# A scan and a mixture of adapters: a written order of every engine in place of a planner's, with deeper rings

## The chip, the cores and the metric

The kernel runs on one core of a Trainium2 chip. The time is that of the device, in microseconds, for one execution from inputs in HBM to the output in HBM. The profile is of one execution, and its span runs from the first to the last instruction of the program.

The engines are named as in the profile: PE (TensorE, matmuls and transposes), PEld (its weight loads), DVE (VectorE), ACT (ScalarE), POOL (GpSimd) and SP (SyncE, which issues the DMAs here). Each has a queue of its own that runs strictly in order, and they meet only through semaphores.

## What is computed

```python
# a, b: (8, 6400, 128), f32; 51200 rows of 128 in all
h = 0                                   # for each of the 8 batches
for t in range(6400):
    h = a[:, t] * h + b[:, t]
    x[:, t] = h
x = x.reshape(51200, 128)
logits = x @ w_gate                     # w_gate (128, 8)
topk = two largest logits of each row   # weights: softmax over the two
delta = sum over the two e of  weight * (x @ A[e]) @ B[e]   # A (8,128,16), B (8,16,128)
out = x + delta
```

## The kernel before

The 51200 rows are cut into 100 units of 512 rows. A unit goes through these operations, named by letter and unit in the code:

- **lda, ldb** (SP): loads of a and b, 512 KB for two units, into rings of 8 slots (16 units); a pairs units 2k-1 and 2k, b pairs 2k and 2k+1. A load waits until the transposes of the units that held its slot are done.
- **AB** (PE, line 86): 8 + 8 transposes of a and b, f32 with half of the array, into PSUM tiles pA (one buffer) and pB (two). The units 0, 1 and 99 have them in two halves, A and AB.
- **aev** (ACT, line 491): pA to SBUF (a_st). **scan** (DVE, line 510): the recurrence along the free dimension, from a_st and pB into xT, a ring of XR = 16 units in f16, transposed (128 features on the partitions).
- **L** (PE, line 82): logits, into a part of the PSUM tile pTL. After a group of up to four units **lev** (ACT, line 583) takes them out, and the gating chain **m1, p1, p2, p3, m2, p4, p5, p6, p7** (DVE for m, POOL for p) and **sig** (ACT, line 684) makes the weights g. The first three groups have a short form (mx, p4, p1, p5, p6, p7) whose p steps may run on POOL or DVE.
- **Z** (PE, pZ), **mul** (DVE, line 729; 21 of 100 on POOL after a copy **zev** by ACT): x A, times the weights, into zw.
- **T** (PE, into the other part of pTL) and **tev** (ACT, line 786): zw transposed, in zwT (4 units).
- **R** and **D** (PE, pO, two buffers): x by the identity, plus zwT by B, added up in one PSUM tile.
- **oev** (ACT, line 821; for the last ten units ACT or DVE): pO into outt, a ring of NOUT = 24 slots.
- **st** (SP): stores of 512 KB for a pair, numbers 2 to 48; the units 0, 1 and 96 to 99 have stores of 256 KB, numbers 0, 1 and 49 to 52. Store j of a pair holds the units 2j-2 and 2j-1. A store waits for its oev, and, where its first unit u is below 78, for the scan of unit u + 22 (HOLD, FREE).

The order of each queue is made when the kernel is built: `_Plan.schedule` is a list scheduler with costs in nanoseconds for each operation, a table of offsets (KEY) that sets priorities, and a slack for each engine. From about unit 24 on, the order that it makes on PE is regular: `AB60 T48 L58 D46 Z51 R47 AB61 T49 ...`, so T runs 12 units behind AB, D 14 and R 13. On DVE a round of four units is `scan mul scan mul m scan mul scan m`. On SP each pair of loads is followed by one store once stores begin (store 0 after the load of b for unit 38). Its last part is `ldb98 st31 lda99 st32 st33 st34 st35 st36 st40 st37 st41 st42 st38 st43 st39 st44 ... st52`. The last queue entry waits for all stores of the end.

The waits that an operation has are kept with it (`deps`), and `_Plan.run` writes for each a wait on the semaphore of the engine that it needs, its own engine included. Two of them bear on the change:

```python
[f"AB{w}", f"aev{w}"] + [f"scan{w - 1}"] + [f"{k}{v}" for v in mates(w - XR) for k in "RDZL"]   # scan
[f"D{v}", f"st{store_of.get(v - NOUT)}"]                                                        # oev
```

## Time and profile before

| | |
|---|---|
| three runs, us | 204.41, 206.39, 206.44 (median 206.39) |
| the profiled execution, us | 204.88 |
| its span, us | 203.1 |
| instructions | 8757 |
| HBM read and written, MB | 52.56 and 26.21 |
| mean granted TensorE clock | 0.989 |
| scan (DVE), each | 1252 ns, 96 whole ones |
| product (DVE) / product (POOL), each | 679 / 1060 ns |
| evacuations by ACT: aev, tev, oev, each | 606, 615, 626 ns |

Busy times of DVE and ACT contain the last part of an instruction in which the next one has begun, so that the durations add up to more than the time they take in a row. Busy PE is modelled in the profile, as its matmuls are pipelined: what counts there is when the next instruction begins and whether it waited.

### The profile page before, as it was taken

The numbers are of one execution on the slowest core, as the hardware profiler recorded it, in microseconds if no ns is written. First come the engines' busy times: TensorE is split into PE (matmuls) and PEld (weight loads), VectorE is DVE, ScalarE is ACT, GpSimd is POOL, SyncE is SP. The second block draws the span as 40 slices with busy tenths as digits, with TensorE's granted clock in tenths as the row PEclk, the third lists the DMA queues.
The fourth block names the chain that finished last, engine by engine and source line by source line (L and its number), as shares of the span: only waits on it lengthen the run. The fifth ranks groups of instructions, "written<-read, shape, count | busy, mean of one in ns | idle before, by whom it ended". The sixth has DMA issues, their size and how long they took to land.

```text
span 203.1 us, 8757 instructions
## 1 busy us (share of the span) xinstructions
PE 191.2 (94%) x3591; PEld 172.3 (85%) x3591; DVE 184.8 (91%) x268; ACT 173.7 (86%) x383; POOL 115.7 (57%) x244
## 2 busy tenths in 40 slices
PE   7788888999999999999999999999999999999992
PEld 3666777879899999999999999999999999999981
DVE  1579989999999999999999999999999999989970
ACT  3157686869899999989999999999999999999883
POOL 1324427568567466565656746656565687875520
PEclk9799999999999999999999999999999999999999
DMA  7999999999999999999999999999999999988867
GB/s 182 402 410 408 403 409 405 404 412 404 404 414 412 416 412 410 413 408 416 414 408 416 410 412 416 410 414 414 409 411 414 414 416 409 372 330 345 324 250 279
DMA packets 23688, 79.35 MB, mean 391 GB/s; under 512 B 3681, under 2 KB 3809, under 8 KB 23649
## 3 DMA queue, kind: packets, MB, share of 16 engines
q1 hardware_dynamic: 22320, 78.65, 97.0%
q8 instruction: 29, 0.48, 0.9%
q10 hardware_dynamic: 1328, 0.14, 0.5%
q14 instruction: 11, 0.08, 0.1%
HBM read 52.56 MB, written 26.21 MB: 388 GB/s over the span
## 4 chain that ended last, share of the span: by engine, by line
PE 81%; DVE 6%; ACT 6%; DMA 2%; issue 2%; POOL 1%; SPq 0%; DVEq 0%
PE pA L86 26%; PE pO L82 23%; PE pTL L86 14%; PE pZ L82 10%; PE pTL L82 5%; DVE xT L510 4%; PE pB L86 4%; DMA a_in<-in_a_dram 2%; ACT a_st L491 2%; ACT outt L821 2%; ACT zwT L786 1%; DVE mx L589 0%; SPq L311 0%; DVE zw L729 0%; ACT z_sb L715 0%
## 5 line engine op out<-in xcount | busy, mean ns | idle before, releaser
L510 DVE TENSOR_TENSOR_SCAN xT<-a_st,xT,pB 128x512 f16<-128x512 f32 x96 | 120.2, 1252 | 4.4 <-PE pZ L82 1.1
L491 ACT COPY a_st<-pA 128x512 f32<-128x512 f32 x100 | 60.6, 606 | 20.4 <-PE pB L86 15.7
L86 PE MATMUL pA<-ident_f,a_in 64*128 64x64 f32 (+1 forms) x792 | 71.8, 230 | 3.3 <-DMA a_in<-in_a_dram 1.1
L86 PE MATMUL pB<-ident_f,b_in 64*128 64x64 f32 (+1 forms) x792 | 72.5, 232 | 0.2
L86 PEld LDWEIGHTS pA<-ident_f,a_in 64*128 64x128 f32 (+1 forms) x792 | 58.0, 139 | 11.6 <-issue 2.4
L821 ACT COPY outt<-pO 128x512 f32<-128x512 f32 x96 | 59.5, 626 | 1.9 <-PE pO L82 1.7
L786 ACT COPY zwT<-pTL 128x512 f16<-128x512 f16 x95 | 58.4, 615 | 1.0 <-PE pTL L86 1.0
L86 PEld LDWEIGHTS pB<-ident_f,b_in 64*128 64x128 f32 (+1 forms) x792 | 58.0, 140 | 0.7 <-DMA b_in<-in_b_dram 0.4
L729 DVE TENSOR_TENSOR zw<-pZ,g 128x512 f16<-128x512 f32 x79 | 53.2, 679 | 2.1 <-PE pTL L86 1.2
L82 PE MATMUL pO<-ident_h,xT 128*128 128x128 f16 x400 | 41.2, 229 | 0.9 <-ACT outt L821 0.9
L82 PE MATMUL pZ<-cst_h,xT 128*128 128x128 f16 x400 | 38.6, 221 | 0.0
L86 PE MATMUL pTL<-ident_h,zw 128*128 128x128 f16 x380 | 37.7, 222 | 0.4 <-ACT zwT L786 0.4
L82 PE MATMUL pO<-cst_h,zwT 128*128 128x128 f16 x400 | 36.9, 218 | 0.6 <-ACT zwT L786 0.4
L82 PEld LDWEIGHTS pO<-ident_h,xT 128*128 128x128 f16 x400 | 32.8, 148 | 1.6 <-ACT outt L821 1.2
L729 POOL TENSOR_TENSOR zw<-z_sb,g 128x512 f16<-128x512 f32 x21 | 22.3, 1060 | 17.6 <-PE pTL L82 17.2
L82 PE MATMUL pTL<-cst_h,xT 128*128 128x8 f16 x400 | 27.9, 175 | 1.6 <-DVE xT L510 1.3
L82 PEld LDWEIGHTS pZ<-cst_h,xT 128*128 128x128 f16 x400 | 28.1, 115 | 0.2
L86 PEld LDWEIGHTS pTL<-ident_h,zw 128*128 128x128 f16 x380 | 21.8, 98 | 6.4 <-ACT zwT L786 0.5
L82 PEld LDWEIGHTS pTL<-cst_h,xT 128*128 128x128 f16 x400 | 23.6, 117 | 2.9 <-DVE xT L510 1.8
L625 POOL TENSOR_TENSOR d<-Lg,m 128x128 f32<-128x128 f32 (+3 forms) x29 | 10.7, 368 | 26.6 <-DVE m L618 26.5
L82 PEld LDWEIGHTS pO<-cst_h,zwT 128*128 128x128 f16 x400 | 23.9, 98 | 1.0 <-PE pO L82 0.9
L660 POOL TENSOR_SCALAR pn<-d 128x128 f32<-128x128 f32 (+3 forms) x31 | 17.3, 557 | 2.7
(36 smaller groups left out, 137.2 us busy)
## 6 DMA issues: line engine op xcount, KB each, us to landing
a_in<-in_a_dram SPq DMA_DIRECT2D x49, 512.0 KB, 13.7
b_in<-in_b_dram SPq DMA_DIRECT2D x49, 512.0 KB, 13.5
out_dram<-outt SPq DMA_DIRECT2D x47, 512.0 KB, 13.1
out_dram<-outt SPq DMA_DIRECT2D x6, 256.0 KB, 2.7
a_in<-in_a_dram SPq DMA_DIRECT2D x2, 256.0 KB, 9.2
b_in<-in_b_dram SPq DMA_DIRECT2D x2, 256.0 KB, 4.3
cst_f<-in_moe_A_dram ACTq DMA_DIRECT2D x1, 64.0 KB, 4.0
cst_f<-in_moe_B_dram ACTq DMA_DIRECT2D x1, 64.0 KB, 5.0
```

What stands on the lines that cost most here:

```text
L82: return self.h.matmul(*args, **kw)
L86: return self.h.transpose(*args)
L491: lambda h: h.copy(a_st[w % 2][:, :], pA[0][:, :]),
L510: last = h.tensor_tensor_scan(out=x_at(lo, hi), data0=a_st[w % 2][:, lo:hi], data1=pB[w % 2][:, lo:hi], initial=init, op0=ALU.mult, op1=AL ...
L625: lambda h: h.tensor_tensor(out=v(d1[s]), in0=v(Lg[s]), in1=bc(m1[s]), op=ALU.subtract),
L660: lambda h: h.tensor_scalar(v(pn[s]), v(d2[s]), 0.0, -1.0e30, ALU.is_lt, ALU.mult),
L729: lambda h: h.tensor_tensor(out=oview, in0=zview, in1=gview, op=ALU.mult),
L786: lambda h: h.copy(*evacuated(v)),
L821: return copy(outt[:, v % NOUT, :], pO[v % NO][:, :])
```

## The change

The scheduler goes, with its costs, offsets and slacks. In its place stand five strings with a letter for each operation, one for each engine, and two that give the order in which the users of the PSUM tiles pA and pTL hold them. The n-th letter of a kind is the n-th operation of that kind.

```diff
-KEY = {
-    "AB": -228.9, "aev": 79.1, "scan": 140.1, "L": -12.2, "lev": -63.6, "gate": 83.5, "sig": 69.7, "Z": 27.8,
...
+ORDERS = {
+    "pe": """
+        hAaAaLaLZaZRaZLLaTRLaZTaDLaTaZDLLLaZaTRaZaTDLRaDRLLLaTRLZaDZTaDTZLaRLLDaRZDaTLLRaZTLRaLDTZaZDRTaRZLT
...
+    "sp": """
+        jiijjijjijiiiijjijjjjijiijjiijiiijjiiijjjjiiwwjijiijwijwwjjjiiwiiwwiwiwijjiwiwjiijjjijjjwwwwwiwjjiiii
+        wijiwijwiwwwwwjjjjjiijwijwiwwwwwjwjwiwwwwwwwwwwwwwwwwwwe
+    """,
 }
...
+ELSE = "oev90 oev94 oev97 oev98 oev99 p4_0 p5_0 p5_1".split()
...
-XR = 16
-NOUT = 24
+XR = 20
+NOUT = 36
...
+    def arrange(self):
+        ops = list(self.ops.values())
+        for op in ops:
+            op.deps = [self.ops[d] for d in dict.fromkeys(op.deps) if d in self.ops]
+        self.order = {e: self.pick(ORDERS[e], [op for op in ops if op.eng == e]) for e in self.sems}
...
-        zwT = [sb(nc.sbuf_tensor(f"zwT{i}", [128, 2 * UT], F16)) for i in range(2)]
+        zwT = [sb(nc.sbuf_tensor(f"zwT{i}", [128, 4 * UT], F16)) for i in range(2)]
...
-            deps = [f"aev{w - 1}", f"scan{w - 2}", "id"]
+            deps = [f"aev{w - 1}", f"scan{w - 2}", "id", "heat"]
...
-                [f"T{v}"] + [f"D{w}" for w in mates(v - 4)],
+                [f"T{v}"] + [f"D{w}" for m in mates(v) for w in mates(m - 8)],
...
-        plan.schedule(700.0, 3000.0, lambda t: 400.0, 94.0)
+        plan.arrange()
```

The letters of PE: h the heating matmuls, A and a the transposes, the others as above; of SP: i lda, j ldb, w a store. ELSE names the operations that may run on two engines and run on DVE here: the evacuations 90, 94, 97, 98 and 99 (before: 90, 92, 94 and 97) and the gating steps p4_0, p5_0 and p5_1 (before: p7_0, p7_1, p7_2 and p5_2). The 21 products on POOL are those of the same units, now in a list.

Read with their numbers, some parts of the new orders:

- PE, beginning: `heat A0 AB0 A1 AB1 L0 AB2 L1 Z0 AB3 Z1 R0 AB4 Z2 L2 L3 AB5 T0 R1 L4 AB6` (before: `heat A0 AB0 A1 L0 AB1 Z0 R0 AB2 L1 Z1 R1 AB3 L2 AB4 T0 Z2 AB5 L3 D0 AB6`).
- PE, middle: `AB40 D24 R25 Z30 T28 L37 L38 AB41 D25 R26 Z31 T29 L39 L40 AB42 R27 D26 T30 D27 Z32 Z33 AB43 R28 L41 T31 D28 AB44`.
- DVE, beginning: `scan0 scan1 mx_0 p4_0 p5_0 scan2 mx_1 mul0 scan3 p5_1 scan4 mx_2 mul1` (before: `scan0 mx_0 scan1 p7_0 scan2 mul0 mx_1 scan3 p7_1 scan4 mul1 mx_2`).
- DVE, end: `scan98 mul88 m1_30 mul89 mul90 mul91 m2_30 scan99 mul92 mul93 m1_31 oev90 mul94 mul95 m2_31 mul96 mul97 oev94 mul98 mul99 oev97 oev98 oev99` (before: `mul88 m2_29 scan97 mul89 mul90 m1_30 scan98 mul91 m2_30 scan99 mul92 mul93 m1_31 oev90 mul94 mul95 m2_31 oev92 mul96 mul97 oev94 mul98 mul99 oev97`).
- ACT, end: `oev93 sig31 tev96 oev95 tev97 oev96 tev98 tev99` (before: `oev93 tev96 tev97 sig31 oev95 oev96 tev98 tev99 oev98 oev99`).
- SP: the first loads are b, then a, of unit 0 (before a, then b). Loads and stores come in runs: `lda71 ldb68 ldb70 ldb72 st12 st13 st14 st15 st16 lda73 st17`, `lda87 ldb80 st20 lda89 st21 st22 st23 st24 st25 ldb82 ldb84 ldb86 ldb88 ldb90`. The end is `lda97 st28 ... st32 ldb96 st33 ldb98 st34 lda99 st35 st36 ... st52`, the stores in the order of their numbers.

## The prediction

> **What bounds the kernel now.** The page comes first, for the share of each engine and for the chain of waits.

> ```profile
> span 203.1 us, 8757 instructions
> PE 191.2 (94%) x3591; PEld 172.3 (85%) x3591; DVE 184.8 (91%) x268; ACT 173.7 (86%) x383; POOL 115.7 (57%) x244
> PE 81%; DVE 6%; ACT 6%; DMA 2%; issue 2%; POOL 1%; SPq 0%; DVEq 0%
> ```

> TensorE, VectorE and ScalarE are all near full, and 81% of the chain runs on TensorE. An average hides the stages, so the busy time by stretches is next. Its columns are the stretch and its length, busy time (instructions) of each engine, the granted clock, the share of the DMA engines and the GB/s.

> ```profile
> 0.00:5.00 5.00, 3.63 (x12) 1.52 (x13) 0.56 (x3) 1.66 (x3) 0.89 (x7) 1.00 0.70 179
> 5.00:10.00 5.00, 3.92 (x42) 3.38 (x44) 3.04 (x7) 1.09 (x3) 1.61 (x6) 0.76 1.03 401
> 10.00:50.00 40.00, 35.25 (x669) 30.37 (x666) 37.57 (x63) 29.23 (x67) 20.41 (x49) 0.99 1.03 407
> 50.00:180.00 130.00, 129.84 (x2576) 119.86 (x2574) 127.35 (x170) 123.95 (x274) 83.83 (x161) 1.00 1.02 410
> 180.00:190.00 10.00, 9.84 (x169) 9.15 (x170) 9.29 (x14) 9.45 (x23) 6.22 (x16) 1.00 0.87 346
> 190.00:203.06 13.06, 8.72 (x136) 8.01 (x136) 6.98 (x13) 8.35 (x18) 2.72 (x8) 0.97 0.69 266
> ```

> From 10 to 50 us VectorE is the fuller engine (2.43 us idle) and PE idles 4.75 us. From 50 to 180 us PE idles 0.16 us and VectorE 2.65 us. The DMA engines run at 407 to 410 GB/s until 180 us and then slacken. The waits of the middle stage, and the beginnings of the transposes of two neighbouring units, say which engine sets the pace there.

> ```profile
> POOL d L625 <- DVE m L618: 20.5, 17, 1.5
> POOL zw L729 <- PE pTL L82: 16.7, 17, 1.1
> ACT a_st L491 <- PE pB L86: 5.2, 20, 0.6
> DVE xT L510 <- ACT a_st L491: 0.4, 2, 0.2
> 100.27 0.27 PE L86 MATMUL pA<-ident_f,a_in 64*128 64x64 f32 x1
> 102.08 0.27 PE L86 MATMUL pA<-ident_f,a_in 64*128 64x64 f32 x1
> ```

> The same view kept to PE lists no wait at all between 50 and 180 us; the others wait for PE. A unit takes 102.08 - 100.27 = 1.81 us, and 100 units make 181 us. So the span of 203.06 us is about 181 us of PE issue, and 22 us of beginning, of stalls up to 50 us, and of the end. DMA needs this:

> ```profile
> q1 hardware_dynamic: 22320, 78.65, 97.0%
> out_dram<-outt SPq DMA_DIRECT2D x47, 512.0 KB, 13.1
> out_dram<-outt SPq DMA_DIRECT2D x6, 256.0 KB, 2.7
> ```

> 78.65 MB at 410 GB/s are 191.8 us, so DMA is nearly as tight as PE. A last store of 256 KB takes 2.7 us, of which 0.262 MB at 410 GB/s are 0.64, so about 2.06 us are fixed.

> **The change, part by part.** No operation is added or removed on PE, ACT or SP except that a few evacuations and gating steps change engine; the same 21 products stay on POOL. What moves is the order, and the depth of three rings. So the middle cannot gain while PE issues 1.81 us a unit without a wait. What can move is the beginning, the stalls, and the end.

> *Beginning.* These are VectorE's first rows.

> ```profile
> 5.61 1.22 DVE L510 TENSOR_TENSOR_SCAN xT<-a_st,pB 128x512 f16<-128x512 f32 x1 [3.88 <-PE pB L86]
> 8.07 0.37 DVE L589 MAX8 mx<-Lg 128x8 f32<-128x8 f32 x4 [1.25 <-ACT Lg L583]
> 8.50 1.28 DVE L510 TENSOR_TENSOR_SCAN xT<-a_st,xT,pB 128x512 f16<-128x512 f32 x1
> 9.76 0.19 DVE L674 TENSOR_TENSOR um<-d,pn 128x32 f32<-128x32 f32 x1
> 11.08 1.28 DVE L510 TENSOR_TENSOR_SCAN xT<-a_st,xT,pB 128x512 f16<-128x512 f32 x1 [1.13 <-PE pZ L82]
> ```

> Two gaps, 1.25 and 1.13 us, stand before scan 1's max and before scan 2. Today PE runs L0 between A1 and the second half of unit 1, and Z0, R0 ahead of AB2. The new order runs A1, AB1, L0, AB2, and only then L1 and Z0; VectorE runs scan 0 and scan 1 back to back and then mx_0. That takes Z0 and R0 out of the way of scan 2. Against it stand the swap of the first two loads and the new wait of A0 for the end of the heating matmuls: both delay scan 0 (A0 and B0, now one after the other behind the second load; 0.262 MB at 410 GB/s put that load 0.64 us behind). Scan 0 has the 1.25 us gap behind it, so this is covered; without the gap it would cost those 0.64 us. The steps p4_0, p5_0 and p5_1 come to VectorE and p7_0 to p7_2 and p5_2 leave it, at 0.19 us each by the row of p7: 0.19 us less work. The bounds of the whole head are a loss of 0.64 and a gain of 2.38 us (both gaps); I take half the gaps, 1.2 us, since the next loads are still only landing then.

> *Middle.* The written order is less regular: groups of two to five L stand together, and R and D come in pairs. On PE a stall is lost time, as every other engine waits for it. A loss of 0 is the bound from the row 50 to 180 us (0.16 us idle); the other is the idle share of 10 to 50 us, 4.75 in 40, which over 130 us would be 15.4 us. The same operations with the same distances between producer and user (T still runs 12 units behind AB) are near the first, and x of 20 units instead of 16 loosens the one wait that was tight: scan w waits for R, D, Z and L of units w-16 and w-15, and D45 stands today right before AB60. I take a loss of 0.6 us, about one stall.
> [...]

> *Loads and stores.* SP's queue is in order, so each DMA waits for what stands before it. The tightest new place is the load of b for unit 82. It now stands behind a's load for unit 89, which needs AB74 done, and behind stores 20 to 25. From AB74 to AB82 are 8 x 1.81 = 14.5 us; lda89, six stores and the load itself are 8 x 0.524 MB, 10.2 us at 410 GB/s, plus 2.06 us. It lands with some 2 us to spare: nothing, as long as the queue is empty when it starts; with one more store ahead of each it would cost up to a unit. 36 slots instead of 24 cost and bring nothing by themselves: no ACT wait for a store stands among the waits, and oev v now waits for the store of v-36.

> *End.* These rows are VectorE's, with POOL and ScalarE where the last gate comes from.

> ```profile
> 185.83 1.27 DVE L510 TENSOR_TENSOR_SCAN xT<-a_st,xT,pB 128x512 f16<-128x512 f32 x1
> 188.01 1.28 DVE L510 TENSOR_TENSOR_SCAN xT<-a_st,xT,pB 128x512 f16<-128x512 f32 x1
> 189.20 1.26 DVE L729 TENSOR_TENSOR zw<-pZ,g 128x512 f16<-128x512 f32 x2
> 194.29 0.32 POOL L674 TENSOR_TENSOR um<-d,pn 128x64 f32<-128x64 f32 x1
> 195.27 0.60 ACT L786 COPY zwT<-pA 128x512 f16<-128x512 f16 x1
> 195.74 0.28 ACT L684 ACTIVATE g<-um 128x64 f32<-128x64 f32 x1
> 196.05 1.29 DVE L729 TENSOR_TENSOR zw<-pZ,g 128x512 f16<-128x512 f32 x2 [0.74 <-ACT g L684]
> 197.70 0.69 DVE L821 COPY outt<-pO 128x512 f32<-128x512 f32 x1 [0.35 <-PE pO L82]
> 199.36 0.58 ACT L821 COPY outt<-pO 128x512 f32<-128x512 f32 x1 [0.16 <-PE pO L82]
> ```

> The last gate (sig 31) waits in ACT's queue behind tev96 and tev97 although its input is there at 194.61; in the new order it stands before tev96. VectorE also loses oev92 before the last products and takes oev98 and oev99 behind them. The products of units 98 and 99 waited 0.74 us for the gate: that goes (-0.7), and the last evacuation takes 0.69 instead of 0.58 us (+0.1). Together -0.6 us.

> A new order of stores ends with 35, 36 ... 52. Store 39 holds units 76 and 77 and waits for scan 98 (HOLD 22); today 40 to 43 go ahead of it or beside it, in the new order 39 to 52 all stand behind that wait. These are ten of 512 KB and four of 256 KB, 6.29 MB, 15.3 us at 410 GB/s, plus 2.06 us: the end cannot come before scan 98's end + 17.4 us. Scan 98 ends today at 185.83 + 1.27 = 187.10, and the span 16.0 us later, so with scan 98 where it is this would cost 1.4 us. But VectorE's new order has mul88, mul89, mul90 and m1_30 behind scan 98 that stand before it today, 3 x 0.63 (half a row of two) + about 0.19 = 2.1 us. So scan 98 is at 187.1 - 2.1 - 1.2 + 0.6 = 184.4 us.

> **Sum.** By the engines: 203.06 - 1.2 + 0.6 - 0.6 = 201.9 us. By the stores: 184.4 + 17.4 = 201.8 us. The profiled execution took 204.88 us for its span of 203.06, 1.82 us more; 201.8 + 1.82 = 203.6 us. The profiled time is 0.7% below the median of 206.39 and near the lowest of the three (204.41), so against the median this is 1.4% less, and against the profiled execution 0.6%.

> **The rivals.** *Nothing is won.* The head gives nothing, as the loads set it, and the stores take the end: 187.1 - 2.1 + 0.6 + 17.4 = 203.0 us, 204.8 us in time. For it: DMA's share of 1.03 from 5 us on. Chance 0.22.

> *VectorE closes its gaps.* If PE's modelled 100% is not a limit, deeper rings let VectorE run on: its 2.65 us of idle time in 50 to 180 us go, and the loss of 0.6 does not come: 203.06 - 1.2 - 2.65 - 0.6 = 198.6 us, 200.4 us in time. For it: weight loads busy 119.86 of 130 us. Against it: PE's empty list of waits. [...] Chance 0.15.

> *Slower: PE stalls in the middle.* Its place is PE's queue between 50 and 180 us: an operation stands ahead of its input, and all behind it wait. The chain of the written order crosses engines that are 95% (ACT) and 98% (VectorE) busy there, so a late evacuation is not made up. At 0.46 us in 10, a bit under half of what 10 to 50 us show (4.75 in 40), the price is 6.0 us: 203.06 - 1.2 - 0.6 + 6.0 = 207.3, 209.1 us in time. It decides from 1.8 us on, the saving of head and end. Chance 0.23.

> **How the numbers follow.** The forecast has 0.40. Within 1% is what a measurement of this kernel cannot tell from no change, since its three runs lie 1% apart; faster by 1% is under 204.3, slower over 208.5 us. The forecast's 203.6 lies 0.7 us inside faster: 0.30 of its 0.40 there, 0.10 within. VectorE's rival gives 0.15 faster; the one of no gain 0.03 faster, 0.19 within. The stalls give 0.19 slower and 0.04 within, as a price of 3 us would be 206.1. Moving 0.01 to slower for a load that comes late, that is 0.48, 0.32 and 0.20. The range goes from 199.8 (the second rival, with a little more of the head) to 208.6 us (most of the stalls); it leaves out some 0.1 at either end.

> **What would show it.** Right: VectorE's gaps before scans 1 and 2 shrink by about 1.2 us; PE idles under 1 us between 50 and 180 us with a unit still at 1.81 us; scan 98 ends near 184.4 us; SP issues stores without a pause behind it, at about 410 GB/s; products 98 and 99 wait no longer for the gate. Wrong: PE waits listed in the middle; a unit under 1.79 us; loads of b near unit 82 awaited by PE; a DMA rate in the last 17 us below 380 GB/s.

## The result, and the profile after

The changed kernel takes **206.12 us** (median of 20 runs, 205.03 to 209.6) where the kernel before, run beside it on the same chip, takes 204.41 us (median of 20, 204.18 to 206.44). The ratio of the mean times is 1.0069, with a 95% interval of 1.0040 to 1.0097; it leaves out the three longest runs of the changed kernel (208.27 to 209.60 us), which fell in a slower state of the chip. That is slower, by less than the 1% that the prediction called no change, but not by nothing. The forecast was 203.6 us. The 206.39 us that it was measured against was the median of only three runs: of the 20 here, three lie at 206.4 us and the others from 204.2 to 204.9. Against 204.41 us the forecast was 0.4% less, a change inside the prediction's own band of no change. The profiled execution took 205.23 us, 0.35 us more than that of before.

These are lines of the page of the changed kernel:

```profile
span 203.4 us, 8803 instructions
PE 191.5 (94%) x3591; PEld 171.9 (85%) x3591; DVE 184.2 (91%) x268; ACT 177.5 (87%) x383; POOL 115.9 (57%) x245
PE 87%; DMA 3%; ACT 3%; DVE 3%; issue 2%; SPq 1%; DVEq 0%
```

The busy times are within 1 us of those of before, but for ScalarE's, which is 3.8 us more; the chain lies still more on PE (87% for 81%), with 3% of DMA in it (2% before). The busy time by stretches, with the columns that the prediction explains, shows where things moved:

```profile
5.00:10.00 5.00, 4.02 (x45) 3.23 (x45) 2.77 (x7) 2.79 (x6) 0.29 (x1) 0.89 1.04 405
10.00:50.00 40.00, 36.70 (x708) 32.15 (x706) 39.43 (x65) 31.58 (x71) 22.75 (x57) 0.97 1.03 407
50.00:180.00 130.00, 128.68 (x2531) 118.12 (x2529) 124.12 (x169) 124.54 (x270) 82.31 (x156) 1.00 1.02 406
180.00:190.00 10.00, 9.94 (x178) 9.33 (x177) 9.22 (x14) 9.53 (x22) 6.83 (x19) 1.00 0.77 301
190.00:203.40 13.40, 8.77 (x136) 7.93 (x135) 8.07 (x14) 7.79 (x18) 2.84 (x8) 1.00 0.85 329
```

From 10 to 50 us VectorE idles 0.57 us in place of 2.43, and PE 3.30 in place of 4.75: the beginning did get shorter. From 50 to 180 us PE idles 1.32 us in place of 0.16: something was lost there. The waits of PE in that stage, which were an empty list before, are now this one, and the timeline of PE has its place (start, duration, instruction, and in brackets the idle time before it):

```profile
PE pA L119 <- DVE xT L433: 1.2, 1, 1.2
```

```profile
151.81 0.25 PE L119 MATMUL pA<-ident_f,a_in 64*128 64x64 f32 x1 [1.16 <-DVE xT L433]
```

The instruction is the first transpose of unit 82. The view names VectorE, but the scan that the transposes wait for, that of unit 80, had ended at 150.23 us; the load of b for units 82 and 83 landed at 151.68 us, 0.13 us before the transposes began. Here is the queue ahead of it, in SP's timeline (neighbours of one kind are one line, with their count at the end):

```profile
133.36 0.33 SPq L287 DMA_DIRECT2D a_in<-in_a_dram  x1
133.74 0.44 SPq L287 DMA_DIRECT2D b_in<-in_b_dram  x1
134.28 0.41 SPq L287 DMA_DIRECT2D out_dram<-outt  x1
136.97 0.33 SPq L287 DMA_DIRECT2D a_in<-in_a_dram  x1
137.40 2.78 SPq L287 DMA_DIRECT2D out_dram<-outt  x5
140.22 3.88 SPq L287 DMA_DIRECT2D b_in<-in_b_dram  x5
```

Each transfer reports sixteen completions in the trace; the last of them is its landing, and these are worked out from there:

| transfer | lda87 | ldb80 | st20 | lda89 | st21 | st25 | ldb82 |
|---|---|---|---|---|---|---|---|
| issued, us | 133.36 | 133.74 | 134.28 | 136.97 | 137.40 | 139.49 | 140.22 |
| landed, us | 140.11 | 141.37 | 142.67 | 144.25 | 145.56 | 150.46 | 151.68 |

When lda89 is issued, five transfers are still under way (lda85, st19, lda87, ldb80 and st20), and from lda87 on every next one lands 1.2 to 1.6 us after the one before it. So ldb82 is not late by its own cost but by its place in a line that is never empty. A later run has the same order of SP with most of the stores' bytes left out (stores 2 to 48 light, below): there ldb82 lands 5.19 us after its issue, where it takes 11.45 here, and nothing waits for it.

At the end, SP issues as predicted, from 184.42 us on, when scan 98 has ended (184.35 us; the prediction had 184.4):

```profile
184.42 15.72 SPq L287 DMA_DIRECT2D out_dram<-outt  x14
```

The DMA issues after 198.4 us, with their size and the median time from issue to landing, first of before, then of after:

```profile
out_dram<-outt SPq DMA_DIRECT2D x3, 256.0 KB, 2.3
```

```profile
out_dram<-outt SPq DMA_DIRECT2D x3, 256.0 KB, 3.1
```

The last evacuation ends at 199.78 us (before 199.94), so the engines are 0.16 us ahead; the last store then takes 3.09 us to land (issued 199.81, landed 202.90) instead of 2.21. From the last landing to the end of the span are 0.53 us (before 0.89).

### The profile page after: what moved, and what is told of

Same layout as the page of the kernel before. It is cut to its first block, busy times and chain, and to the rows that moved or that the text cites. A ratio compares the mean times of both kernels' runs of the same rounds, so it can differ in the third digit from the quotient of the medians.

```text
span 203.4 us, 8803 instructions
## 1 busy us (share of the span) xinstructions
PE 191.5 (94%) x3591; PEld 171.9 (85%) x3591; DVE 184.2 (91%) x268; ACT 177.5 (87%) x383; POOL 115.9 (57%) x245
## 3 DMA queue, kind: packets, MB, share of 16 engines
q1 hardware_dynamic: 22320, 78.65, 97.4%
## 4 chain that ended last, share of the span: by engine, by line
PE 87%; DMA 3%; ACT 3%; DVE 3%; issue 2%; SPq 1%; DVEq 0%
PE pA L119 29%; PE pO L115 26%; PE pZ L115 12%; PE pTL L119 11%; PE pTL L115 6%; PE pB L119 3%; DMA b_in<-in_b_dram 3%; ACT a_st L414 2%; DVE xT L433 1%; SPq L287 1%; DVE outt L688 1%; DVE zw L610 1%; ACT zwT L659 1%; ACT outt L688 0%; DVE mx L495 0%
## 5 line engine op out<-in xcount | busy, mean ns | idle before, releaser
L414 ACT COPY a_st<-pA 128x512 f32<-128x512 f32 x100 | 60.0, 600 | 13.2 <-PE pB L119 9.8
L659 ACT COPY zwT<-pTL 128x512 f16<-128x512 f16 x95 | 57.2, 602 | 1.9 <-PE pTL L119 1.2
L688 ACT COPY outt<-pO 128x512 f32<-128x512 f32 x95 | 57.3, 605 | 0.7 <-PE pO L115 0.6
L115 PE MATMUL pO<-ident_h,xT 128*128 128x128 f16 x400 | 42.7, 231 | 0.0
L115 PE MATMUL pO<-cst_h,zwT 128*128 128x128 f16 x400 | 38.7, 220 | 0.4 <-ACT zwT L659 0.2
L115 PEld LDWEIGHTS pO<-cst_h,zwT 128*128 128x128 f16 x400 | 24.6, 98 | 3.3 <-PE pO L115 0.9
L119 PEld LDWEIGHTS pTL<-ident_h,zw 128*128 128x128 f16 x380 | 24.3, 98 | 1.6 <-issue 0.3
L115 PE MATMUL pTL<-cst_h,xT 128*128 128x8 f16 x400 | 23.6, 174 | 0.2 <-DVE xT L433 0.2
L115 PEld LDWEIGHTS pTL<-cst_h,xT 128*128 128x128 f16 x400 | 20.6, 117 | 1.1 <-DVE xT L433 0.2
## 6 DMA issues: line engine op xcount, KB each, us to landing
a_in<-in_a_dram SPq DMA_DIRECT2D x49, 512.0 KB, 10.8
b_in<-in_b_dram SPq DMA_DIRECT2D x49, 512.0 KB, 11.5
out_dram<-outt SPq DMA_DIRECT2D x47, 512.0 KB, 10.3
out_dram<-outt SPq DMA_DIRECT2D x6, 256.0 KB, 3.6
b_in<-in_b_dram SPq DMA_DIRECT2D x2, 256.0 KB, 4.1
a_in<-in_a_dram SPq DMA_DIRECT2D x2, 256.0 KB, 8.5
```

What stands on the lines that cost most here:

```text
L115: return self.h.matmul(*args, **kw)
L119: return self.h.transpose(*args)
L414: lambda h: h.copy(a_st[w % 2][:, :], pA[0][:, :]),
L659: lambda h: h.copy(*evacuated(v)),
L688: return copy(outt[:, v % NOUT, :], pO[v % NO][:, :])
```

## Experiments

Five theories are told apart, under the letters that the expectations use. **A**: the late load of b for unit 82 took the gain. **B**: the irregular orders of the engines cost time in the middle by themselves. **C**: the new order of stores, held back to scan 98, sets the end. **D**: the DMA engines are full from the first microseconds to the end, so that the slowest of the sixteen sets the landing of late loads and last stores, and a moment in which they run dry, or a transfer in the wrong place, isn't made up. **E**: the engines, or the mean DMA rate, set the end. Each result is a median with its runs, and the ratio to the kernel before in runs on the same chip (204.38 to 204.42 us).

**The late load and the stores' wait.** Three kernels: the five loads b 82 to 90 moved ahead of stores 21 to 25; FREE lowered from 100 to 92, which frees the stores of units 70 to 77 from waiting for a scan; both.

```diff
-        wijiwijwiwwwwwjjjjjiijwijwiwwwwwjwjwiwwwwwwwwwwwwwwwwwwe
+        wijiwijwijjjjjwwwwwiijwijwiwwwwwjwjwiwwwwwwwwwwwwwwwwwwe
```

```diff
-FREE = 100
+FREE = 92
```

> Only change from the changed kernel: on SP the five loads of b for units 82 to 90 stand ahead of stores 21 to 25 instead of behind them. Theory A (a late load ate the gain): PE's wait of 1.2 us before AB82 at 151.8 us goes and nothing takes its place; span 203.4 - 1.2 = 202.2 us, median about 205, and the runs scatter less. Rival B (the middle's irregular order costs in itself, load or no load): the wait goes but PE's lead over the kernel before still melts, span 203.0 us or more. Rival C (the stores set the end): scan 98 ends 1.2 us earlier, but the last landing moves under 0.5 us.

> Only change: FREE 92 instead of 100, so that stores 36 to 39 no longer wait for scans 92 to 98. Theory C (the stores set the end): the queue is empty at the end again, the last store lands 2.2 us after its issue as before instead of 3.1, span 202.6 us. Theory A alone: the engines' end does not move, so 0 to -0.7 us, and the wait before AB82 is there as in the changed kernel.

> Both edits. A and C: 203.4 - 1.2 - 0.7 = 201.5 us in the span, a median near 203.5, under the kernel before. B: 202.5 us or more.

Measured: the load first 205.35 us (204.30 to 208.54, 13 runs; 1.0034, 1.0018 to 1.0049); FREE alone 206.63 (205.57 to 208.05, 6; 1.0104, 1.0071 to 1.0136), with the wait for unit 82 still there; both 205.38 (204.84 to 206.72, 7; 1.0050, 1.0015 to 1.0086). So the load is worth 0.8 us by the medians (by the ratios 0.7, with intervals that overlap), and FREE nothing or less: in the changed kernel freeing these stores is no gain, though in its profile the last store lands 2.04 us after its issue, as C had it. The sum of A and C, 203.5 us for both, did not come. The kernel with both tells why so little came of it. No wait of PE for a load is left in its middle, and its last evacuation ends at 198.62 us, 1.16 us earlier than in the changed kernel. But this is its last store:

```profile
out_dram<-outt SPq DMA_DIRECT2D x1, 256.0 KB, 3.6
```

Issued at 198.65, it lands at 202.26 us. The engines end earlier, and the stores take the gain back.

**SP's order alone, both ways.** The changed kernel with the SP order of before, given as a list of names; and the kernel of before, planner and all, with 36 output slots and the SP order of after.

```diff
+        plan.order["sp"] = [plan.ops[n] for n in SP_NAMES.split()]
```

> The changed kernel with the whole order of SP from the kernel before; PE, VectorE, ScalarE and POOL keep their written orders, x 20 units and 36 slots. A and C: all that the written order lost was lost in SP's queue, so 201.5 us or less, and a scatter like that of the kernel before. B: the written orders of the engines lose the middle in any case, 203 us or more.

> The kernel before, every other engine by its planner, with the order of SP of the changed kernel and 36 output slots. If SP's order is what costs (A, C, D): 205 to 207 us and a scatter of 2 us or more. If the written orders of the other engines cost (B): as the kernel before, 204.4 us with its small scatter.

Measured: 204.44 us (204.34 to 204.60, 11; 1.0001, 0.9992 to 1.0010) and 211.63 us (211.24 to 214.32, 6; 1.0361, 1.0303 to 1.0419). All of the loss of the changed kernel lies in SP's order: without it the written orders of the four engines tie with the planner's. They do not win either: the profile has 202.8 us of span, where A and C had 201.5. Beside engines that it was not written with, the same SP order costs 7.2 us, more than the 205 to 207 us that were expected. There the DMA engines do run dry, as the first row (180 to 190 us) of its stretches says, and PE waits for a load:

```profile
180.00:190.00 10.00, 10.00 (x189) 9.33 (x186) 9.12 (x14) 9.50 (x24) 6.55 (x18) 1.00 0.44 174
190.00:209.40 19.40, 11.85 (x185) 10.84 (x184) 10.25 (x18) 11.37 (x24) 5.31 (x13) 0.91 0.83 326
```

```profile
PE pA L96 <- DMA b_in<-in_b_dram: 2.4, 1, 2.4
```

What holds the stores back is in the list of SP's own waits (L208 is the line that writes an operation's waits):

```profile
SPq L208 <- DVE xT L520: 25.4, 8, 4.4
```

Stores 35 to 39 are issued 3.4 to 4.8 us apart, each when its scan has ended. Scan 98 ends at 190.42 us here, store 39 goes out at 190.49, and the last of the 14 stores from it on lands 18.4 us later, at 208.91; in the changed kernel these 14 take 18.5 us, from 184.42 to 202.90. So in this kernel it is C, the stores held back to scan 98, that sets the end.

**Fewer bytes in the middle.** Stores 20 to 27 write 16 of their 128 partitions, 3.7 MB less, in the kernel with both repairs and in that of before; part of the output is left out.

```diff
+            if j in LIGHT:
+                dst, src = dst[0:16], src[0:16]
```

> The kernel with both edits (loads of b 82 to 90 ahead of the stores; FREE 92), and stores 20 to 27 write only 16 of their 128 partitions: 3.7 MB less, and that part of the output is missing. Theory D (the slowest of the 16 DMA engines never runs dry, and its last packet is the end, though the mean share falls to 0.7): there the last store landed 3.6 us after its issue; with less to move it lands 2.2 us after it, and the span is 1.3 us under the 203.1 us of the kernel with both edits, about 201.7 us. Theory E (PE and the chain of engines set the end): 203.1 us, no change.

> The kernel before with the same 3.7 MB left out of stores 20 to 27. Its last store landed 2.2 us after its issue, so there the engines end as late as the DMA queue: D and E both say no change, 203.0 us within 0.3. If it gets faster by 1 us or more, the queue was late for the engines elsewhere too.

Measured: 203.86 us (203.16 to 206.22, 12; 0.9962, 0.9931 to 0.9993) and 203.94 us (203.73 to 206.36, 12; 0.9977, 0.9940 to 1.0014). The first lost 1.5 us as D had it, and its last store lands 2.02 us after its issue. The second was to stay as it was and came out 0.5 us shorter. Its interval just holds no change, because two of its runs lie at 206.3 us; the other ten, 203.73 to 204.23, lie below all 23 runs of before beside them (204.24 at the least). So before is held by the same line of transfers, only less, which neither D nor E had.

**The DMA engines alone.** The changed kernel with SP's order of before, without logits, gates, products and D: PE, VectorE and ScalarE only transpose, scan and copy out x.

> The changed kernel with the order of SP of the kernel before, and all of logits, gating, products and adapters left out (the output is the scan alone): every load and store stays, PE keeps 20 of 36 matmuls a unit. D: the span falls only to the floor of the slowest DMA engine. Between the landings of the first pair of a and the last load of a the kernel before moved 67.6 MB in 169.0 us, 400 GB/s; 6.5 us + 77.6 MB / 400 GB/s + 0.9 = 201 us; with fewer instruction fetches 200 us. E: far under it, 1.65 + 78.65 MB / 410 GB/s + 2.9 = 196.4 us.

Measured: 200.10 us (199.92 to 200.30, 4; 0.9765, 0.9711 to 0.9819). Its stretches:

```profile
180.00:190.00 10.00, 4.89 (x32) 2.88 (x32) 2.76 (x4) 2.90 (x5) 0.00 (x0) 0.50 1.03 419
190.00:198.40 8.40, 0.00 (x0) 0.00 (x0) 0.00 (x0) 0.00 (x0) 0.00 (x0) 0.50 0.56 220
```

With PE half idle the DMA engines stay full to 190 us, and the span is still 198.4 us. That lies between D and E (200 to 201 and 196.4 us expected): moving the bytes takes 198.4 us, 5.0 us less than the span of the changed kernel. The transfers alone do not set the end either.

**The engines alone.** Stores 2 to 48 write 16 of their 128 partitions (about 21 MB less; part of the output is left out): the changed kernel's engines with SP's order of before, the kernel of before, and the changed kernel whole.

```diff
+LIGHT = range(2, 49)
```

> The changed kernel's engine orders with the SP order of before, and stores 2 to 48 write only 16 of their 128 partitions (part of the output is left out): about 21 MB less, so that the DMA engines have some 50 us of slack. D (the engines' new order is faster, and the saturated DMA engines hide it): with the DMA engines out of the way the gain of the head reaches the end, the span is 200.0 to 201.0 us, at least 0.8 us below the kernel of before with the same light stores. B (the new engine orders bring nothing over the whole length): as that kernel, within 0.4 us.

> The kernel of before with the same light stores 2 to 48 (part of the output is left out). It is the end that before's engines set by themselves. With eight light stores it had 202.2 us of span. D and B: 201.5 to 202.3 us here, as its engines then follow their own pace; lower than 201 would say that the DMA engines held before's engines back over the whole length too.

> The changed kernel whole, its own SP order included, with stores 2 to 48 light (part of the output is left out). If SP's order costs only because the DMA engines then run dry for a moment that they cannot make up (D), it costs nothing here: within 0.4 us of the same kernel with SP order of before. If a load behind a waiting store on SP stalls the engines by itself, it stays 0.8 to 1.7 us above that kernel, as it is with full stores (206.1 against 204.4 us).

Measured: 203.18 us (202.92 to 203.64, 4; 0.9932, 0.9907 to 0.9956), 203.79 us (203.25 to 207.29, 10; 0.9966, 0.9943 to 0.9990) and 202.99 us (202.60 to 203.71, 4; 0.9915, 0.9890 to 0.9941). With room on the DMA engines SP's order of after costs nothing, and the new orders are 0.6 to 0.8 us faster than the planner's by the medians. The kernels with new orders have four runs each, and the intervals overlap, so the size is loose; the gain looks smaller than 1.2 us. Between the changed kernel and the same with light stores lie 3.1 us, and 0.6 us for the kernel of before. That is about what each pays for full DMA engines.

**Load and end apart.** Only stores 33 to 48 light (part of the output is left out), first in the changed kernel, then with b 82 to 90 moved ahead too; and, with nothing left out, b 82 to 90 ahead and b 10 two places earlier. (The first row of SP's string stands here as the kernel has it; where the change was shown above, it has a letter too many, `wijww` for `wjww`.)

```diff
+LIGHT = range(33, 49)
```

```diff
-        jiijjijjijiiiijjijjjjijiijjiijiiijjiiijjjjiiwwjijiijwjwwjjjiiwiiwwiwiwijjiwiwjiijjjijjjwwwwwiwjjiiii
+        jiijjijjijiijijiijjjjijiijjiijiiijjiiijjjjiiwwjijiijwjwwjjjiiwiiwwiwiwijjiwiwjiijjjijjjwwwwwiwjjiiii
```

> The changed kernel whole, with only stores 33 to 48 light (part of the output is left out): they are issued behind the last loads, so that every load meets the same queue as in the changed kernel, and only the end is freed. It parts the 3.1 us between the changed kernel (206.12 us) and the same with stores 2 to 48 light (202.99 us). If all of it is the wait for late loads (A): 206 us, within 0.3. If all of it is the end that is full of transfers (D at the end): 203.0 us. If both, 1.2 us of load wait and the rest at the end: 204.0 to 204.6 us.

> The changed kernel with the loads b 82 to 90 ahead of stores 21 to 25, and stores 33 to 48 light (part of the output is left out): the two single repairs together, which brought 0.8 us (205.35) and 0.7 us (205.44) from 206.12. If they add up: 204.6 us, and the 1.6 us that are left to the kernel with stores 2 to 48 light (202.99) sit in further loads. If the load and the end are one fault, each hiding the other: 203.0 to 203.8 us. If loads other than b 82 hold the engines just as well: 205.2 us or more.

> The changed kernel with the loads b 82 to 90 ahead of stores 21 to 25, and at the head a 7, a 9, b 10, a 11, b 12, a 13 in place of a 7, a 9, a 11, a 13, b 10, b 12, as before wrote them: b 10 landed at 22.8 us and was wanted 0.1 us later. Nothing of the work is left out. If this late load is what was left in the loads: 204.4 to 204.9 us against 205.35 with b 82 alone. If not: 205.2 to 205.5 us.

Measured: the end freed alone 205.44 us (204.41 to 208.62, 10; 1.0056, 1.0024 to 1.0087); with the load ahead as well **203.34 us** (202.95 to 204.97, 10; 0.9949, 0.9918 to 0.9980); b 82 and b 10 205.04 us (204.23 to 207.18, 10; 1.0023, 0.9988 to 1.0058). The load ahead brings 0.8 us and the freed end 0.7, which alone is inside the noise (ratio 1.0056 beside 1.0069), and both together bring 2.8, by the ratios 1.2% (0.9949): each fault hides the other. With the end free, PE still waits for the load of b 82, landed at 151.96, and as long as 1.71 us:

```profile
152.10 0.24 PE L120 MATMUL pA<-ident_f,a_in 64*128 64x64 f32 x1 [1.71 <-DVE zw L611]
```

Its last evacuation ends at 200.12 us, but the last store needs only 2.04 us. With both repairs the middle lists no wait of PE, and these are its stretches from 180 us on (the span ends at 201.24) and its last store:

```profile
180.00:190.00 10.00, 9.93 (x172) 9.35 (x169) 9.12 (x15) 9.53 (x24) 6.63 (x17) 1.00 0.35 48
190.00:203.40 13.40, 7.63 (x118) 6.92 (x118) 6.99 (x12) 6.73 (x14) 2.13 (x6) 0.87 0.34 100
```

```profile
out_dram<-outt SPq DMA_DIRECT2D x1, 256.0 KB, 2.0
```

Four profiles side by side, in us, make the parts plain (PE's step is from the beginning of the transposes of unit 80 to those of unit 82; two units are 3.62):

| kernel | PE, unit 80 to 82 | last evacuation ends | last store: issue to landing | span |
|---|---|---|---|---|
| after | 4.84 | 199.78 | 3.09 | 203.43 |
| b 82 ahead and FREE 92 | 3.62 | 198.62 | 3.61 | 203.15 |
| end free | 5.40 | 200.12 | 2.04 | 202.72 |
| b 82 ahead and end free | 3.61 | 198.63 | 2.04 | 201.24 |

Moving b 10, which had landed 0.15 us before its use, changed nothing that could be measured (205.04 beside 205.35). No full kernel came out faster than that of before: the one with its SP order ties, and the others stay above.

## Why the prediction was wrong, step by step

**The step that failed** is the one on loads and stores: "It lands with some 2 us to spare: nothing, as long as the queue is empty when it starts." The queue was not empty. The sum gave the load 10.2 + 2.06 = 12.3 us from the moment at which lda89 can be issued; that was 136.97 us, and 149.2 us would have been in time for unit 82, at 150.5. But lda85, st19, lda87, ldb80 and st20 were still moving, lda89 took 7.28 us to land where 2.06 + 1.28 = 3.34 were reckoned, and the load landed at 151.68, 2.4 us after the sum. (Of the 3.9 us by which lda89 was late, 1.3 are store 20, which the sum had counted among its six.) Such a backlog was in a row that the prediction itself quoted: a store of 512 KB took a median of 13.1 us from issue to landing, where store 39 of after, which met an almost empty line, took 3.17. The condition was stated, and its price ("up to a unit") came true: 1.2 us in the profiled execution of after, 1.7 in that with the end free. It should have been the forecast. Two of the signs of being wrong that the prediction lists came with it: a load of b near unit 82 that PE waits for, and a DMA rate under 380 GB/s at the end (301 and 329).

**"The DMA engines run at 407 to 410 GB/s until 180 us and then slacken"** was the second wrong reading, of the same kind. The mean share falls after 180 us, to 0.87 before and 0.77 after, but the transfers of 512 KB keep landing one after the other, 1.2 to 1.7 us apart in both (but for one pause of 2.55 in after); some of a transfer's sixteen completions come while others are far behind: those of the load of a for unit 99, before, run from 168.91 to 175.54 us, 6.6 us. The GB/s show this no better, as they fell with the share (301 in that stretch). Where the last store is late, it is late by one or two of its sixteen completions alone:

| the last store's completions, us after its issue | 14th | 15th | 16th |
|---|---|---|---|
| before | 2.16 | 2.16 | 2.21 |
| after | 2.03 | 2.40 | 3.09 |
| b 82 ahead and FREE 92 | 2.01 | 2.04 | 3.61 |
| b 82 ahead and end free | 1.99 | 2.00 | 2.04 |

**The beginning** gained about what was forecast, but not where it was forecast. VectorE's order became what was told. The two gaps are gone or small, but scan 0 starts at 6.46 us for 5.61, and a new gap of 0.73 us stands ahead of scan 1. These are its first scans, after:

```profile
6.46 1.22 DVE L433 TENSOR_TENSOR_SCAN xT<-a_st,pB 128x512 f16<-128x512 f32 x1 [1.75 <-PE pB L119]
8.41 1.28 DVE L433 TENSOR_TENSOR_SCAN xT<-a_st,xT,pB 128x512 f16<-128x512 f32 x1 [0.73 <-ACT a_st L414]
10.58 1.28 DVE L433 TENSOR_TENSOR_SCAN xT<-a_st,xT,pB 128x512 f16<-128x512 f32 x1 [0.18 <-PE pZ L115]
```

But the gaps of 1.25 and 1.13 us were partly the clock's. In the profiled execution of before, TensorE was granted half its clock there, as one-microsecond stretches show:

```profile
7.00:8.00 1.00, 1.00 (x13) 0.93 (x12) 0.00 (x0) 0.63 (x2) 0.04 (x1) 0.80 1.03 410
8.00:9.00 1.00, 1.00 (x10) 0.94 (x9) 0.87 (x5) 0.04 (x1) 0.45 (x2) 0.50 1.02 410
9.00:10.00 1.00, 1.00 (x17) 0.80 (x17) 0.95 (x2) 0.00 (x0) 0.58 (x2) 0.50 1.02 410
10.00:11.00 1.00, 1.00 (x18) 0.88 (x15) 0.00 (x0) 0.59 (x2) 0.00 (x0) 0.50 1.03 410
11.00:12.00 1.00, 0.96 (x21) 0.73 (x18) 0.92 (x1) 0.20 (x2) 0.00 (x0) 0.99 1.04 414
```

In the kernel of before with light stores, whose beginning is the same, the slow clock lies ahead of scan 0: its first four transposes, from 4.18 us on, begin 0.21 us apart, where those of before begin 0.11 apart, and from 6.5 us on it has the full clock. There scan 0 starts at 6.51 us, and the gaps are 0.61 and 0.18 us:

```profile
8.35 0.37 DVE L590 MAX8 mx<-Lg 128x8 f32<-128x8 f32 x4 [0.61 <-ACT Lg L584]
8.64 1.27 DVE L511 TENSOR_TENSOR_SCAN xT<-a_st,xT,pB 128x512 f16<-128x512 f32 x1
10.40 1.28 DVE L511 TENSOR_TENSOR_SCAN xT<-a_st,xT,pB 128x512 f16<-128x512 f32 x1 [0.18 <-ACT a_st L492]
```

Both gaps together are 0.79 us there, not 2.38: their size hangs on where the slow clock falls. The changed kernel with both faults taken away begins as the changed kernel does, and it has the full clock from 5.2 us on:

```profile
6.36 1.22 DVE L434 TENSOR_TENSOR_SCAN xT<-a_st,pB 128x512 f16<-128x512 f32 x1 [1.63 <-PE pB L120]
8.30 1.28 DVE L434 TENSOR_TENSOR_SCAN xT<-a_st,xT,pB 128x512 f16<-128x512 f32 x1 [0.73 <-PE pB L120]
10.32 1.28 DVE L434 TENSOR_TENSOR_SCAN xT<-a_st,xT,pB 128x512 f16<-128x512 f32 x1
```

Scan 2 starts at 10.32 us, 0.08 earlier than with the old order, though that has the full clock on record only from 6.5 us: the two gaps were worth next to nothing. The gain comes behind them: scan 16 starts at 33.84 us for 35.28. These are the busy times of both from 0 to 50 and from 0 to 150 us, first the old order with light stores, then the new one with both faults taken away:

```profile
0.00:50.00 50.00, 43.03 (x730) 35.35 (x731) 41.78 (x73) 32.84 (x74) 23.51 (x63) 1.00 0.99 384
0.00:150.00 150.00, 142.92 (x2713) 127.57 (x2713) 139.88 (x201) 128.09 (x280) 85.24 (x173) 1.00 0.96 351
```

```profile
0.00:50.00 50.00, 43.19 (x757) 35.67 (x758) 42.88 (x74) 35.71 (x77) 24.08 (x65) 1.00 0.99 382
0.00:150.00 150.00, 143.06 (x2720) 127.45 (x2721) 139.34 (x200) 132.44 (x282) 86.07 (x176) 1.00 1.01 397
```

Up to 50 us PE has begun 757 matmuls for 730. A unit has 36 of them and takes 1.81 us, so the new order is 1.4 us ahead. That the forecast had 1.2 is luck, as its place was wrong; whether the order or the deeper rings bring it was not tried.

**The middle** was to lose 0.6 us to stalls. Without the late load none is listed, and yet PE is a little slower per unit there. By 150 us the lead has shrunk to 7 matmuls (2720 for 2713), 0.35 us. From 60 to 160 us the mean step from one operation to the next, added up over AB, L, Z, T, R and D, is 1810 ns in the kernel of before with light stores, and 1823 and 1829 in the two kernels of the new orders with the same: 13 to 19 ns by some 55 units are 0.7 to 1.0 us. That is B in a small measure, and near the forecast size, though not by stalls; which operation pays is not settled. The rival of PE stalls at 6.0 us did not come, nor did VectorE's: with the DMA engines free PE was as full as before (129.93 of 130 us from 50 to 180 us with SP's order of before and light stores, 129.84 in the profile of before).

**The end** went as told in its order and not in its size. The last products no longer wait for the gate, but the evacuation ahead of them now waits for PE:

```profile
195.01 0.69 DVE L688 COPY outt<-pO 128x512 f32<-128x512 f32 x1 [0.49 <-PE pO L115]
195.61 1.28 DVE L610 TENSOR_TENSOR zw<-pZ,g 128x512 f16<-128x512 f32 x2
```

From the end of scan 99 to that of the last evacuation are 10.48 us after and 10.65 before: 0.2 us won, where 0.6 were forecast.

The 14 stores stand behind scan 98 as told. It ended within 0.1 us of the forecast, which is luck: without the late load it ends at 183.16 us. The bound by the stores, 184.4 + 17.4 = 201.8 us, fell short by 1.6 us. Store 39 landed 3.17 us after its issue and the last four as reckoned, but the nine stores 40 to 48 took 12.8 us for a reckoned 11.5: store 45 landed 2.55 us after store 44, as one of its sixteen completions came 1.15 us behind the fifteenth (196.70 for 195.55). The other 0.5 us lie between the last landing and the end of the span, which the sum put at nothing. The 2.06 us in it came from a median of six stores; the last store of before, alone, took 2.21 us and not 2.7.

The bound by the engines, 201.9 us of span, is near what the kernel with both faults taken away has (201.2), but again not by its terms: the profile that the sum starts from had lost some 0.8 us to the clock, as the last section works out. Beside the kernel of before with light stores (201.93 us of span) the new orders win 0.7 us, where the sum had 1.2, and 0.37 of it by the last evacuation (198.63 for 199.00). So the engines gained less than was forecast, and the transfers took more than that away. The rival "nothing is won" was the nearest of the cases, with 203.0 us of span, and its reason, a DMA share of 1.03 from 5 us on, was the right one, though the beginning did give something. It got 0.22 and should have led.

That the changed kernel's median lies 0.9 us above its own profiled execution fits the late load: without the three longest its runs scatter over 2.8 us, those with b 82 ahead, taken the same way, over 1.6, and those with SP's order of before over 0.26. The mean granted clock does not order them (207.43 us at 0.999, 205.22 at 0.992). That the wait for b 82 is longer in the longest of them was not seen, as only profiled executions show waits.

## What to carry to other kernels

Where the DMA engines are full, price a moved transfer by what is in flight when it is issued; the median time from issue to landing against that of a nearly empty line (here 13.1 against 3.2 us) gives that backlog in one row. Take such faults away together before judging any of them: here two changes of 0.8 and 0.7 us, one of which left out part of the output, were worth 2.8 us together. And a gap that a change is to close should be checked in a second execution, or against the granted clock of its own microsecond, before it is counted as the order's.

## What the runs showed of the hardware

Bytes alone do not give the time here: with 78.65 MB to move in both, the DMA engines ran at 414 GB/s from 50 to 180 us in the kernel without logits and gates (share 1.03), and at 406 in the changed one (share 1.02). That kernel also had 16 fetches of instructions in place of 29, of 16 KB each; whether they make the difference was not tried. In the kernel with both faults taken away, such a fetch runs from 190.65 to 191.77 us, and the sixteenth completion of store 45 comes 1.32 us behind its fifteenth (0.02 us for store 44, 0.03 for store 46). The trace does not tell on which engine a packet ran, so that the fetch is what holds one engine back is suggested and not shown; in the changed kernel one runs at 193.68 us, ahead of the pause at store 45.
